# A Gram matrix from 64-column products over cyclic pairs of blocks, with one block copied by GpSimd, and an earlier load

## Chip, cores, metric

One core of a Trainium2 chip. The metric is the device time of one execution in microseconds; the kernel before takes 166.79 us in the median. Engine names in the profile lines: PE is TensorE (PEld its weight loads), ACT is ScalarE, DVE is VectorE, POOL is GpSimd, SP is SyncE. Lines such as L616 are lines of the kernel that the trace belongs to, so the same piece of code has different numbers in different kernels.

## The reference, cut to what matters

```python
# attention stand-in: a causal convolution of 7 taps over the sequence, one filter per group of 24 features
y   = conv(x, softmax(weight))                    # x: 8 batches x 4224 tokens x 192 features
# token mixer without a nonlinearity between tokens
wq, wk = y @ w_q, y @ w_k                         # 192 -> 64
W_tok  = einsum('bsd,btd->bst', wq, wk) / 8
out    = relu(W_tok @ y) @ w_out
```

Since nothing nonlinear stands between the tokens, `W_tok @ y` is `wq @ (w_k^T (y^T y)) / 8`. So the kernel needs, per batch, the Gram matrix `y^T y` (192 x 192, symmetric), its product M with w_k, the projection q of y, then `relu(q M) @ w_out`. All matmuls are in bf16.

## The kernel before

The kernel is one straight-line program. A batch has 4224 tokens; two halves of 18 chunks of 128 rows, 122 of them new. Per batch TensorE does: Y, the convolution with a banded matrix (16 matmuls of 432 columns); G, the Gram matrix, 18 chunks; Q, the projection in small tiles, from a DVE transpose of y; M; Z, `relu` input (12 matmuls of 512 columns); O, the output product. ACT and DVE move every result out of PSUM, the memory that the matmuls write into; I call such a move an eviction.

A Gram chunk, both halves in one go. Features are laid out so that three matmuls with 192, 192 and 128 columns give all blocks that are needed:

```python
    def job_g(b, c):
        def pe(e, bk):
            y = Y[:, b % 2, c, :]
            ...
            e.matmul(PS[:, 7, 0:192], y[:, 0:128], y[:, 0:192], start=c == 0, **fl)
            e.matmul(PS[:, 7, 192:384], y[:, 256:384], y[:, 192:384], start=False, **fl)
            return e.matmul(PS[:, 7, 384:512], y[:, 128:256], y[:, 128:256], start=False, **fl)
```

The last chunk of a batch has invalid rows. They are zeroed by a multiplication with a mask, on ACT or DVE (job YC):

```python
        y = Y[32:64, b % 2, NCK - 1, :]
        ... evacs=[(lambda bk: [(y, y)], ("YC", b), 140, "keep")],
```

The order of instructions on every engine is fixed when the program is built, by a list scheduler in the kernel that keeps a clock of its own. I call that the plan. It has a cost per element for ACT and DVE, and per job on TensorE:

```python
            self.pe_us = sum(max(n, 110) / 2400 + 0.0025 for n in cols)      # TensorE time of a job
    COST = {"act": (0.833e-3, 0.05, 0.16), "dve": (1.04e-3, 0.065, 0.15)}    # per element, gap, latency
            eng = min(COST, key=lambda e_: begin[e_] + n * COST[e_][0] + COST[e_][2])
```

These figures are the constants of the plan. For the evictions the trace of the kernel before agrees: from 432 to 864 columns ACT goes from 526 to 891 ns and DVE from 608 to 1052, that is 0.84 and 1.03 ns per element. The floor of 110 columns it does not show (29 ns from start to start at 64 columns, see below).

The kernel gives each engine its own list and makes it wait for the others by semaphores. The loads of x are issued by GpSimd, each batch in two halves (half loads); those for batches 2 to 7 are at the end of its list, in a ring of 6 batches.

## Time and profile before

| | before |
|---|---|
| median of runs | 166.79 us |
| span of the profiled run | 163.9 us |
| last matmul starts at | 156.5 us |
| 18 Gram chunks of a batch | 18 x 221 ns |
| TensorE idle gaps of 0.3 us or more from 30 to 120 us | 2, 0.85 us together |

The last row is worked out from the trace: start of the next matmul less start of this one, less what this one's columns take back to back. For that I take columns/2.4 + 2.5 ns, which fits the median distances of starts in this trace: 29 ns for 64 columns, 56 for 128, 83 for 192, 163 for 384, 216 for 512. I use it because the recorded matmuls overlap (those of 192 columns are 246 ns long), so that the busy time of PE hides short stops.

The head of the page and the granted clock (TensorE's clock in tenths of full speed, 9 for 90% or more, in 40 slices of the span), of the kernel before:

```profile
span 163.9 us, 4794 instructions
PE 150.9 (92%) x2017; PEld 111.6 (68%) x2017; DVE 122.0 (74%) x241; ACT 129.2 (79%) x235; POOL 51.5 (31%) x86
PEclk9999999999999999999999999999999999999995
```

Groups of TensorE instructions by shape, of the kernel before (line, engine, operation, tiles, shape, count, busy us and mean ns of one, idle before):

```profile
L619 PE MATMUL ps<-y 128*128 128x192 bf16 x144 | 33.8, 246 | 0.3 <-DVE y L884 0.3
L620 PE MATMUL ps<-y 128*128 128x192 bf16 x144 | 33.7, 246 | 0.0
L621 PE MATMUL ps<-y 128*128 128x128 bf16 x144 | 31.5, 219 | 0.0
```

The mean of 246 ns is the recorded length of one matmul. I don't take it for the cost: the next one starts after 83 ns (median), so I go by the distance of starts. The timeline of the kernel before (start us, length us, instruction) has 64-column matmuls, each with its own 128x128 weights, in the product with w_k:

```profile
40.47 0.19 PE L653 MATMUL ps<-gs,wk 128*128 128x64 bf16 x1
40.50 0.19 PE L654 MATMUL ps<-gs,wk 128*128 128x64 bf16 x1
40.53 0.19 PE L655 MATMUL ps<-gs,wk 128*128 128x64 bf16 x1
```

They start 29 ns apart (0.03 in the rounded lines). Busy times by stretch, of the kernel before: length, then busy us of each engine with its number of instructions, granted clock, share of DMA, GB/s.

```profile
25.00:40.00 15.00, 14.46 (x210) 9.84 (x203) 11.23 (x19) 12.79 (x24) 14.05 (x21) 1.00 1.51 214
40.00:60.00 20.00, 19.73 (x259) 14.15 (x259) 16.96 (x31) 18.12 (x33) 15.66 (x23) 1.00 1.41 252
80.00:100.00 20.00, 20.00 (x305) 14.78 (x304) 17.17 (x31) 17.25 (x33) 0.00 (x0) 1.00 1.30 288
```

TensorE is the fullest engine in all three, and GpSimd has nothing left to do after 62 us. The one wait of TensorE for data that is over a microsecond, from the waits view of the kernel before (total us, times, longest):

```profile
PE ps L526 <- DMA xw<-in_x_dram: 1.3, 1, 1.3
```

### The profile page before, as it was taken

How to read it: one execution, taken by the hardware profiler on the slowest of the kernel's cores; microseconds unless marked ns; L12 is line 12 of the kernel's file. 1: busy time of each engine (PE TensorE's matmuls, PEld its weight loads, DVE VectorE, ACT ScalarE, POOL GpSimd, SP SyncE). 2: the span in 40 equal slices, each digit the busy share in tenths (PEclk: the TensorE clock that was granted, in tenths of full speed). 3: DMA queues.
4: the chain of work that ended last, by engine and by line, in shares of the span. 5: the costliest groups of instructions: out<-in, count | busy, mean ns of one | idle time of the engine just before them, and what ended most of it. 6: DMA issues, size and time to landing. Idle time of an engine off the chain costs nothing.

```text
span 163.9 us, 4794 instructions
## 1 busy us (share of the span) xinstructions
PE 150.9 (92%) x2017; PEld 111.6 (68%) x2017; DVE 122.0 (74%) x241; ACT 129.2 (79%) x235; POOL 51.5 (31%) x86
## 2 busy tenths in 40 slices
PE   6899769999999999999999999999999999999920
PEld 5798637575776777777777777677777777867610
DVE  6657846696878898978796989887877987487500
ACT  4544568798999788879997988889996988799940
POOL 7984899989999541000000000000000000000000
PEclk9999999999999999999999999999999999999995
DMA  3999999999999999999999999999993473678996
GB/s 44 186 179 199 145 117 183 193 187 289 214 264 233 332 209 312 341 255 246 278 338 268 272 238 333 289 291 201 363 343 120 177 273 130 219 304 328 356 386 214
DMA packets 47894, 40.37 MB, mean 246 GB/s; under 512 B 37761, under 2 KB 39937, under 8 KB 47873
## 3 DMA queue, kind: packets, MB, share of 16 engines
q0 software_dynamic: 36544, 13.65, 70.3%
q1 hardware_dynamic: 11328, 26.42, 44.4%
q8 instruction: 16, 0.26, 0.6%
q14 instruction: 6, 0.04, 0.1%
HBM read 27.74 MB, written 25.95 MB: 328 GB/s over the span
## 4 chain that ended last, share of the span: by engine, by line
PE 73%; ACT 8%; POOL 7%; DMA 5%; issue 2%; DVE 1%; ACTq 0%; POOLq 0%
PE ps L526 12%; PE ps L733 12%; PE ps L690 11%; PE ps L735 11%; PE ps L591 8%; PE ps L619 7%; PE ps L620 6%; POOL xw L262 5%; DMA xw<-in_x_dram 5%; PE ps L621 4%; ACT o_sb L884 4%; ACT zt L887 2%; ACT y L884 1%; DVE qt L884 1%; PE ps L651 0%
## 5 line engine op out<-in xcount | busy, mean ns | idle before, releaser
L884 ACT COPY o_sb<-ps 128x768 f32<-128x768 f32 (+1 forms) x59 | 45.4, 787 | 7.2 <-PE ps L735 6.5
L884 ACT CAST y<-ps 128x864 bf16<-128x864 f32 (+7 forms) x75 | 42.7, 619 | 6.0 <-PE ps L482 4.2
L888 DVE TENSOR_SCALAR zt<-ps 128x512 bf16<-128x512 f32 x59 | 40.0, 684 | 8.1 <-PE ps L690 7.4
L733 PE MATMUL ps<-wo,zt 128*128 128x192 bf16 x256 | 42.2, 247 | 0.8 <-DVE qt L884 0.5
L262 POOL DMA_DIRECT2D xw<-in_x_dram x50 | 40.2, 817 | 6.7 <-issue 4.3
L735 PE MATMUL ps<-wo,zt 128*128 128x384 bf16 x128 | 41.7, 326 | 0.0
L733 PEld LDWEIGHTS ps<-wo,zt 128*128 128x128 bf16 x256 | 26.9, 114 | 13.0 <-issue 1.6
L882 DVE STREAM_TRANSPOSE yb<-y 128x576 int32<-128x576 int32 x48 | 34.0, 750 | 0.3
L619 PE MATMUL ps<-y 128*128 128x192 bf16 x144 | 33.8, 246 | 0.3 <-DVE y L884 0.3
L620 PE MATMUL ps<-y 128*128 128x192 bf16 x144 | 33.7, 246 | 0.0
L690 PE MATMUL ps<-qt,m_sb 128*128 128x512 bf16 x96 | 33.0, 380 | 0.0
L621 PE MATMUL ps<-y 128*128 128x128 bf16 x144 | 31.5, 219 | 0.0
L526 PE MATMUL ps<-xw,band 128*128 128x432 bf16 x112 | 29.2, 347 | 2.1 <-DMA xw<-in_x_dram 1.3
L884 DVE CAST y<-ps 128x864 bf16<-128x864 f32 (+10 forms) x33 | 19.7, 628 | 7.1 <-PE ps L526 3.9
L887 ACT ACTIVATE zt<-ps 128x512 bf16<-128x512 f32 x37 | 21.6, 619 | 0.6 <-PE ps L690 0.5
L884 ACT CAST qt<-ps 128x576 bf16<-128x576 f32 (+1 forms) x21 | 11.8, 584 | 9.0 <-PE ps L591 9.0
L620 PEld LDWEIGHTS ps<-y 128*128 128x128 bf16 x144 | 14.1, 98 | 6.1
L619 PEld LDWEIGHTS ps<-y 128*128 128x128 bf16 x144 | 14.1, 98 | 5.2 <-issue 1.5
L884 DVE CAST qt<-ps 128x234 bf16<-128x234 f32 (+1 forms) x27 | 10.2, 414 | 9.6 <-PE ps L591 9.6
L591 PE MATMUL ps<-yb,wq 32*64 32x288 bf16 x768 | 15.4, 285 | 0.4 <-ACT y L884 0.4
L526 PEld LDWEIGHTS ps<-xw,band 128*128 128x128 bf16 x112 | 9.2, 97 | 7.8 <-DMA xw<-in_x_dram 1.5
L735 PEld LDWEIGHTS ps<-wo,zt 128*128 128x128 bf16 x128 | 14.5, 113 | 0.0
(79 smaller groups left out, 137.3 us busy)
## 6 DMA issues: line engine op xcount, KB each, us to landing
out_dram<-o_sb SPq DMA_DIRECT2D x31, 768.0 KB, 7.0
xw<-in_x_dram POOLq DMA_DIRECT2D x21, 384.0 KB, 22.8
xw<-in_x_dram POOLq DMA_DIRECT2D x7, 432.0 KB, 21.7
xw<-in_x_dram POOLq DMA_DIRECT2D x4, 240.0 KB, 5.4
out_dram<-o_sb SPq DMA_DIRECT2D x16, 48.0 KB, 5.8
out_dram<-o_sb SPq DMA_DIRECT2D x2, 384.0 KB, 3.6
xw<-in_x_dram POOLq DMA_DIRECT2D x8, 42.0 KB, 10.7
xw<-in_x_dram POOLq DMA_DIRECT2D x1, 336.0 KB, 7.8
```

The lines of the kernel that those rows point to most:

```text
L262: return e.dma_start(XW[lo:hi, b % NX, half, c : c + n, :], bass.AP(x_t, at, [[D, hi - lo], [CW * D, n], [1, D]]),)
L526: last = e.matmul(PS[:, k + j, 0 : 48 * n], BAND[:, h, :], rhs, start=True, stop=True)
L591: last = e.matmul(PS[64 * h : 64 * h + 64, bk + i, 0:288], WQ[r, j, :], rhs, start=j == 0, stop=j == 5, skip_group_check=True)
L619: e.matmul(PS[:, 7, 0:192], y[:, 0:128], y[:, 0:192], start=c == 0, **fl)
L620: e.matmul(PS[:, 7, 192:384], y[:, 256:384], y[:, 192:384], start=False, **fl)
L621: return e.matmul(PS[:, 7, 384:512], y[:, 128:256], y[:, 128:256], start=False, **fl)
L690: return e.matmul(PS[:, bk, :], m[:, parts[k] : parts[k] + 128], q, start=True, stop=True)
L733: e.matmul(o[:, 192 * h : 192 * h + 192], z[:, h, cols], WO1[:, :], start=h == 0, stop=False, **kw)
L735: last = e.matmul(o[:, 0:384], z[:, 2, cols], WO2[:, :], start=False, stop=True, **kw)
L882: return e.transpose(o, i)
L884: return e.copy(o, i) if eng == "act" else e.tensor_copy(o, i)
L888: return e.tensor_scalar(o, i, 0.0, None, op0=ALU.max)
```

## The change

The intent: use the symmetry. With three blocks A, B, C of 64 features, the weights AB, BC and CA, each with its first block as the 64 moving columns, give the six blocks that are needed. Six matmuls of 64 columns replace three of 192, 192 and 128: 384 columns instead of 512. The kernel reads each pair's weights as one run of 128 columns, so for CA it puts a copy of A behind C. That copy (job D, 64 of 192 features) is made by DVE for batches 0 and 1 and by GpSimd afterwards. The mask moves to GpSimd too from batch 2 on. Loads are issued from within the list: three batches up front, then half a batch in front of each copy. The second half load of batch 1 moves ahead of the casts of w_k and w_out.

The core of the diff:

```diff
-    NX = 6
+    NX = 5
+    AHEAD = 3
-    Y = sbuf("y", [128, 2, NCK, 2 * D], BF16)
+    Y = sbuf("y", [128, 2, NCK, 2, YW], BF16)          # YW = 256: 192 features and the copy of 64
     load(1, 0)
+    load(1, 1)
     ...
-            self.pe_us = sum(max(n, 110) / 2400 + 0.0025 for n in cols)
+            self.pe_us = sum(n / 2400 + 0.0025 for n in cols)
     ...                                                 # evictions of y: one piece instead of three
+    def job_dup(b, g):
+        def make(bk):
+            o, i = (Y[:, b % 2, c0:c1, hs, d0 : d0 + 64].rearrange("p c h d -> p h c d")
+                    for d0 in (D, 0))
+            return [(o, i)]
+        return Job(
+            ("D", b, g), ykey(b, c1), 0, None, [],
+            reads=[("Y", b, g, k) for k, q in enumerate(heads) if q[0] < 3]
+            + [("YC", b)] * (c1 == NCK),
+            evacs=[(make, ("D", b, g), 64 * n * len(halves), "dup")],
+        )
     ...
-            e.matmul(PS[:, 7, 0:192], y[:, 0:128], y[:, 0:192], start=c == 0, **fl)
-            e.matmul(PS[:, 7, 192:384], y[:, 256:384], y[:, 192:384], start=False, **fl)
-            return e.matmul(PS[:, 7, 384:512], y[:, 128:256], y[:, 128:256], start=False, **fl)
+            for h in range(2):
+                y = Y[:, b % 2, c, h, :]
+                for k in range(3):
+                    last = e.matmul(
+                        PS[:, 7, 64 * k : 64 * k + 64], y[:, 64 * k : 64 * k + 128],
+                        y[:, 64 * k : 64 * k + 64], ...
     ...                                                 # product with w_k: six matmuls of 64 columns
+    EASY = {"act": 1.0, "dve": 0.3, "pool": 2.0}        # planned cost of copy and mask, relative
     def place(job, t):
+        if kind == "D" and job.name[1] > 1:
+            prefetch(job.name[1] + AHEAD, job.name[2])
+            if what in ("dup", "keep"):
+                if key[1] > 1:
+                    eng = "pool"
```

## The prediction

> What bounds it now. From about 30 to 153 us TensorE is the limit. The busy table by windows gives PE 20.0 of 20 us from 60 to 140 us, ACT 16-18, DVE 16-17.5. Busy PE is no proof, so I read start-to-start times in the timeline: matmuls follow each other at columns/2.4 + 2.5 ns (192 columns 83 ns, 128 56 ns, 512 216 ns), and no gap over 0.45 us is left there. A batch costs 17.5 us (projection bursts of L591 at 70.0, 88.0, 105.1, 122.9 us). Before 30 us the input DMA limits: PE waits 1.3 us for xw at 21.0 us (waits view). After 156.5 us only stores remain, 7 us.
>
> Removed on PE. A Gram chunk is 192+192+128 columns: 83+83+56 = 221 ns. Then it is six 64-column matmuls with a weight load each. The trace has such pairs: L653, L654, L655 and L693 start 29 ns apart with 128x128 weights. So 6 x 29 = 175 ns, 46 less, x18 = 0.83 us per batch. The product with w_k falls from 281 to about 175 ns; the transpose stays. Together 0.93 us per batch. [...]
>
> Removed elsewhere, per batch: the split evictions of one head pair (432+144+288 elements, 0.53+0.29+0.43 us on ACT) become one of 0.89, twice: 0.7 us. The Gram eviction shrinks from 512 to 192 columns: 0.60 to 0.33. The masking of y (0.61 on ACT) goes to GpSimd. About 1.6 us off ACT+DVE (about 30 per batch): they keep pace with the faster PE.
>
> Added. A copy of 1152 elements per half batch: on GpSimd about 1.2 us (estimate from its casts, 288 ns for 128 and 347 for 192 columns)[...]. GpSimd issues loads at 0.5-1.0 us each until 62 us, then idles. The copies wait in its queue behind at most one half load (2.5-3 us), while a batch's Gram starts several us after its y: mostly hidden. [...]
>
> Moved. The second half load of batch 1 is issued at 19.4 us, after the casts; the DMA queue nearly runs dry at 20-22 us. Now it is issued at about 13.7 us, and the casts end about when they did. It should land some 2 us earlier, but PE does not wait for it now, and the wait at 21.0 us is for the first half, which stays. So the Gram saving of batch 0 is lost in that wait, and the move is worth 0 to 1 us. A ring of 5 instead of 6 is still far ahead of need.
>
> Critical path: 7 batches x 0.93 = 6.5 us plus 0.1. Result 160.3 us, 8 in 10 between 158.5 and 162.5. Faster by over 2%: 0.93; within 2%: 0.06; slower: 0.01.
>
> Right if: 64-column Gram matmuls start 29 ns apart; projection bursts of one kind come 16.5-16.7 us apart; PE has no large gaps from 30 us on; GpSimd copies take 1-1.5 us; the wait at 21 us remains, longer.
>
> Wrong if: six weight loads in a row cost more than 29 ns each (37 ns wipes out the gain); PE waits for GpSimd copies around 45-60 us, when loads still fill that queue; DVE becomes slower beside GpSimd; or the earlier load shortens the start by over 1 us.

7 x 0.93 and 0.1 are 6.6 us, which from 166.8 leave 160.2 (put down as 160.3). The distances of starts that the sum rests on are those of the trace of the kernel before, 83, 56 and 29 ns in the median. The queue that nearly runs dry is in its windows view: a DMA share of 0.28 from 20.0 to 20.5 us and 0.03 from 20.5 to 21.0.

## The result, and the profile after

The changed kernel takes 167.74 us in the median (167.47 to 167.91), before 166.79. The ratio is 1.0067, with a 95% interval from 1.0044 to 1.0089: within 2% of before, and a little slower. (Ratios in this text are the mean time of one kernel's fast runs over that of the other's fast runs in the same rounds, so not quite the ratio of the medians quoted.) I had predicted 160.3 us.

The head of the page of the changed kernel:

```profile
span 165.7 us, 5636 instructions
PE 144.4 (87%) x2453; PEld 105.5 (64%) x2453; DVE 120.4 (73%) x231; ACT 124.5 (75%) x212; POOL 74.3 (45%) x104
PEclk9999659999999999999999999999999999999998
```

PE has less to do, and ACT and DVE too, as predicted; the span is longer all the same. So time was lost in waiting. Two groups of the page are new, and one in the groups by shape, of the changed kernel:

```profile
L616 PE MATMUL ps<-y 128*128 128x64 bf16 x864 | 36.7, 195 | 5.3 <-POOL y L890 2.6 <-DVE y L890 2.5
L890 POOL COPY y<-y 128x1152 bf16<-128x1152 bf16 x12 | 13.8, 1153 | 3.8 <-ACT y L890 1.7 <-DVE y L890 1.6
L896 POOL TENSOR_SCALAR y<-y,keep 32x384 bf16<-32x384 bf16 x6 | 7.4, 1240 | 59.1 <-DVE y L890 46.4 <-ACT y L890 12.7
```

The 64-column Gram matmuls start 29 ns apart (median of 801 pairs), so a chunk costs 175 ns as predicted. The copies take 1.15 us each, near the estimate of 1.2. But the Gram matmuls now stand idle for 5.3 us, 5.1 of it behind copies (2.6 on GpSimd, 2.5 on DVE), and the mask takes 1.24 us on GpSimd. Busy times by stretch, of the changed kernel:

```profile
25.00:40.00 15.00, 12.10 (x205) 7.11 (x182) 12.45 (x23) 11.86 (x19) 14.18 (x22) 1.00 1.53 181
40.00:60.00 20.00, 18.31 (x387) 13.60 (x383) 15.81 (x30) 15.27 (x24) 13.77 (x16) 1.00 1.40 258
80.00:100.00 20.00, 17.47 (x307) 12.91 (x307) 14.52 (x27) 15.41 (x26) 6.02 (x6) 1.00 1.35 271
```

In each of these stretches PE is below the value of before. TensorE gaps of 0.3 us or more from 30 to 120 us are now nine, 8.3 us together, where there were two and 0.85 us. I found three kinds.

**The start.** All engines in the timeline of the changed kernel, lines that matter:

```profile
16.11 0.34 PE L616 MATMUL ps<-y 128*128 128x64 bf16 x6
...
17.23 1.44 DVE L888 STREAM_TRANSPOSE yb<-y 128x576 int32<-128x576 int32 x2 [0.53 <-ACT y L890]
17.28 0.61 ACT L896 ACTIVATE y<-y,keep 32x384 bf16<-32x384 bf16 x1
...
18.59 0.45 DVE L890 COPY y<-y 128x448 bf16<-128x448 bf16 x2
...
19.10 0.82 PE L616 MATMUL ps<-y 128*128 128x64 bf16 x12 [2.49 <-DVE y L890]
```

The last two copies of batch 0 wait for the mask (17.28) and stand behind two transposes in DVE's list. The Gram stops for 2.5 us. The record of the granted clock goes to half at 17.42 us and back at 24.25. In the kernel before it stayed full until 160.4 us. The first matmul of Z, which needs the whole Gram matrix of batch 0, starts at 29.05 us instead of 25.06.

**The queue of GpSimd.** The timeline of the changed kernel around 88 us:

```profile
85.90 1.24 POOL L896 TENSOR_SCALAR y<-y,keep 32x384 bf16<-32x384 bf16 x1 [10.99 <-DVE y L890]
...
87.20 1.82 POOL L263 DMA_DIRECT2D xw<-in_x_dram  x2
...
89.01 0.68 POOL L279 DMA_DIRECT2D xw<-in_x_dram  x1
...
89.73 2.42 POOL L890 COPY y<-y 128x1152 bf16<-128x1152 bf16 x2
...
90.93 0.70 PE L616 MATMUL ps<-y 128*128 128x64 bf16 x18 [1.73 <-POOL y L890]
```

y was there at 85.9 us. The copy that the Gram needs was done at 90.9: mask, half a load, copy, one after the other. The same happens at 43.7 us for the first copy on GpSimd, behind the loads of batches 2 to 4 and the first half load of batch 5. Plan and trace disagree there by 11 us: the plan has this copy at 32.7 us, because it counts no time for issuing loads. It starts at 43.58.

**The order of evictions.** Three more stops of about 1 us have no copy in them. The timeline of the changed kernel at 79.5 us:

```profile
79.49 0.25 PE L696 MATMUL ps<-qt,m_sb 128*128 128x64 bf16 x3
79.65 0.80 ACT L890 COPY o_sb<-ps 128x768 f32<-128x768 f32 x1
...
80.51 0.39 PE L693 MATMUL ps<-qt,m_sb 128*128 128x512 bf16 x1 [0.77 <-ACT o_sb L890]
```

The next Z matmul is to go into a PSUM bank that ACT only now empties. It happens at 47.9, 79.5 and 99.4 us (at 99.4 us the profile names an eviction on DVE, `zr`, instead), each time behind the three small matmuls of the last 64 rows (L696).

Theories, as I held them before the experiments: A, the copies and the waits for them ate the gain. B, the new order of work, and evictions in it, leave TensorE idle, copies or not. C, the small matmuls are slow when they go on for long.

### The profile page after: what moved, and what is told of

Its sections match the earlier page's. It is cut to its first block, busy times and chain, and to the rows that moved or that the text cites. A ratio compares the mean times of both kernels' runs of the same rounds, so it can differ in the third digit from the quotient of the medians.

```text
span 165.7 us, 5636 instructions
## 1 busy us (share of the span) xinstructions
PE 144.4 (87%) x2453; PEld 105.5 (64%) x2453; DVE 120.4 (73%) x231; ACT 124.5 (75%) x212; POOL 74.3 (45%) x104
## 3 DMA queue, kind: packets, MB, share of 16 engines
q1 hardware_dynamic: 11472, 26.45, 43.8%
## 4 chain that ended last, share of the span: by engine, by line
PE 55%; POOL 28%; ACT 8%; issue 4%; DVE 2%; ACTq 0%; POOLq 0%
POOL xw L263 18%; PE ps L616 12%; PE ps L693 9%; PE ps L736 9%; PE ps L738 9%; PE ps L517 9%; PE ps L587 6%; ACT o_sb L890 6%; POOL xw L279 2%; POOL y L890 1%; ACT zt L893 1%; POOL wk L790 1%; POOL xw L444 1%; POOL y L896 1%; ACT zr L893 1%
## 5 line engine op out<-in xcount | busy, mean ns | idle before, releaser
L890 ACT COPY o_sb<-ps 128x768 f32<-128x768 f32 (+1 forms) x63 | 47.3, 779 | 4.4 <-PE ps L738 3.5
L890 ACT CAST y<-ps 128x864 bf16<-128x864 f32 (+4 forms) x50 | 39.7, 811 | 10.7 <-PE ps L517 6.6
L894 DVE TENSOR_SCALAR zt<-ps 128x512 bf16<-128x512 f32 x56 | 37.6, 683 | 9.1 <-PE ps L693 9.0
L616 PEld LDWEIGHTS ps<-y 128*128 128x128 bf16 x864 | 33.5, 100 | 14.6 <-POOL y L890 3.2
L616 PE MATMUL ps<-y 128*128 128x64 bf16 x864 | 36.7, 195 | 5.3 <-POOL y L890 2.6
L896 POOL TENSOR_SCALAR y<-y,keep 32x384 bf16<-32x384 bf16 x6 | 7.4, 1240 | 59.1 <-DVE y L890 46.4
L890 DVE CAST y<-ps 128x864 bf16<-128x864 f32 (+3 forms) x22 | 20.5, 933 | 8.2 <-PE ps L517 5.7
L890 DVE CAST qt<-ps 128x234 bf16<-128x234 f32 (+1 forms) x31 | 11.9, 423 | 15.8 <-PE ps L587 15.8
L890 POOL COPY y<-y 128x1152 bf16<-128x1152 bf16 x12 | 13.8, 1153 | 3.8 <-ACT y L890 1.7
L693 PEld LDWEIGHTS ps<-qt,m_sb 128*128 128x128 bf16 x96 | 8.9, 97 | 8.1 <-ACT o_sb L890 1.8
## 6 DMA issues: line engine op xcount, KB each, us to landing
xw<-in_x_dram POOLq DMA_DIRECT2D x21, 384.0 KB, 19.8
```

What stands on the lines that cost most here:

```text
L616: last = e.matmul(PS[:, 7, 64 * k : 64 * k + 64], y[:, 64 * k : 64 * k + 128], y[:, 64 * k : 64 * k + 64], start=c + h + k == 0, stop=c == ...
L693: return e.matmul(PS[:, bk, :], m[:, parts[k] : parts[k] + 128], q, start=True, stop=True)
L890: return e.copy(o, i) if eng == "act" else e.tensor_copy(o, i)
L894: return e.tensor_scalar(o, i, 0.0, None, op0=ALU.max)
L896: return e.mul(o, i, s) if eng == "act" else e.tensor_scalar(o, i, s, None, op0=ALU.mult)
```

## Experiments

Medians and ratios of fast runs. One run of e_late (166.92 us) and one of e_costs_ahead2 (165.56 us) were slow and are left out; with them the medians are 166.24 and 162.13 us. "Before" ran in the same rounds (about 166.1 to 166.4 us in the median in these). I compare the ratios.

| run | median us | ratio to before (95%) |
|---|---|---|
| e_nodup (wrong result) | 161.91 | 0.9752 (0.9698 to 0.9806) |
| e_tiles | 188.56 | 1.1379 (1.1321 to 1.1438) |
| e_dfirst | 165.80 | 0.9998 (0.9941 to 1.0055) |
| e_before_early | 165.74 | 1.0009 (0.9953 to 1.0064) |
| e_start0 | 170.28 | 1.0234 (1.0168 to 1.0300) |
| e_plan | 167.25 | 1.0055 (1.0011 to 1.0100) |
| e_start_dfirst | 163.25 | 0.9809 (0.9752 to 0.9867) |
| e_best2 | 163.76 | 0.9863 (0.9810 to 0.9916) |
| e_late | 165.69 | 0.9951 (0.9855 to 1.0047) |
| e_start | 164.13 | 0.9864 (0.9794 to 0.9934) |
| e_costs_np | 162.08 | 0.9748 (0.9684 to 0.9812) |
| e_late_ahead2 | 165.14 | 0.9920 (0.9842 to 0.9998) |
| e_unmask1 | 170.36 | 1.0236 (1.0182 to 1.0290) |
| e_yc_act | 171.43 | 1.0320 (1.0275 to 1.0366) |
| after_again | 167.75 | 1.0089 (1.0051 to 1.0128) |
| e_costs_ahead2 | 161.83 | 0.9730 (0.9681 to 0.9779) |
| e_costs_d2 | 163.35 | 0.9807 (0.9770 to 0.9845) |
| e_before_costs | 171.10 | 1.0271 (1.0232 to 1.0309) |

A caution for all of them: most edits change what the scheduler sees, and then the order on every engine changes too, and with it which evictions ACT does and which DVE. Only some pairs have the same order on PE, ACT and DVE, so that one thing alone differs: the changed kernel and e_dfirst; e_start and e_start_dfirst; e_start_dfirst and e_late; e_late and e_late_ahead2; e_costs_np and e_costs_ahead2; the kernel before and e_before_early.

### No copies: e_nodup and e_tiles

e_nodup:

```diff
-            evacs=[(make, ("D", b, g), 64 * n * len(halves), "dup")],
+            evacs=[],
-            + [("D", b, g) for g, q in enumerate(GROUPS[b]) if q[1] <= c < q[2]]
-                        PS[:, 7, 64 * k : 64 * k + 64], y[:, 64 * k : 64 * k + 128],
+                        PS[:, 7, 64 * k : 64 * k + 64], y[:, 64 * min(k, 1) : 64 * min(k, 1) + 128],
```

> Wrong result on purpose: the changed kernel without the copies; the third block pair takes columns that are already there as its weights, so TensorE does the same number and shapes of matmuls and nothing waits for a copy. Theory A (the copies and the waits for them ate the gain: the 2.5 us wait at 16.5-19 us, and the waits for GpSimd at 43.7 and 88.9 us): about 160.5 us. Rival B (the new order of work and the evictions, not the copies, leave TensorE idle: the gaps after the small matmuls at 48, 80 and 100 us): 165 to 167 us, with those gaps still there. Rival C (sustained 64-column matmuls are slow): still 167-168 us.

161.91 us. So C falls: the same matmuls are as fast here. The timeline of e_nodup has six of them in 0.34 us at 29.02 us, as long as six take in the changed kernel at 16.11 us. The distance to the changed kernel is 0.9752 against 1.0067, about 5 us of the 7.4 that the prediction missed. It is A together with whatever the other order is worth: none of the stops after the small matmuls is left in this order. The head of the page of e_nodup, and the largest stop that is left in its timeline:

```profile
span 160.7 us, 5636 instructions
PE 144.2 (90%) x2458; PEld 103.8 (65%) x2458; DVE 113.1 (70%) x218; ACT 128.2 (80%) x216; POOL 60.3 (38%) x92
32.38 0.54 PE L517 MATMUL ps<-xw,band 128*128 128x432 bf16 x2 [2.14 <-issue]
```

The profile puts this stop, 2.3 us at 30.0 us by my measure, down to nothing ("issue"); it comes back below. One more of 1.4 us, at 122.8 us, stands behind transposes on DVE.

e_tiles gets the right result without a copy, from two matmuls with 64-column weights:

```diff
+            for h, k, p, q, w in (
+                (0, 0, 0, 128, 0), (0, 1, 0, 128, 64), (1, 0, 0, 128, 0), (1, 1, 0, 128, 64),
+                (0, 2, 0, 64, 128), (0, 2, 64, 128, 0), (1, 2, 0, 64, 128), (1, 2, 64, 128, 0),
+            ):
+                y = Y[:, b % 2, c, h, :]
+                last = e.matmul(PS[p:q, 7, 64 * k : 64 * k + 64], y[:, w : w + q - p],
+                                y[:, 64 * k : 64 * k + 64], ...)
```

> Right result without any copy: the third pair is made by two matmuls with 64-column weights that land in the two halves of the partitions. If two such matmuls run side by side as the projection's small ones do (starts a few ns apart) and changing between full and half-width weights costs nothing, as e_nodup: about 160.5 us under theory A. [...] a chunk costs 0.2 us more, that is 3.6 us per batch: 185 us or more.

The trace of the kernel before shows: the first matmul of a projection burst (64-column weights) starts 149 ns or more after a 128-column Gram matmul, where another full-width one starts after 56, and the first after a burst starts 210 to 212 ns after the last of 288 columns, for which columns/2.4 + 2.5 gives 122. So about 0.1 us for each change of width.

188.56 us. The two half-width matmuls do run side by side (starts 4 ns apart), but the change of width costs: starts in one chunk are 29, 29, 29, 123, 4, 49, 3 and 129 ns apart, 395 ns in all (the median of 85 chunks is 404), where the six of the change take 175. So a change between 128- and 64-column weights costs about 95 to 100 ns each way here (123 and 129 less 29), as at the projection bursts.

### The queue: e_dfirst and e_plan

In e_dfirst the half load is issued after the copy instead of before it:

```diff
-        if kind == "D" and job.name[1] > 1:                 # at the top of place()
-            prefetch(job.name[1] + AHEAD, job.name[2])
+        if kind == "D" and job.name[1] > 1:                 # at its end
+            prefetch(job.name[1] + AHEAD, job.name[2])
```

> The changed kernel, but each GpSimd copy is put ahead of the next half load in GpSimd's queue. Theory A: the copies start 2.5-3 us earlier, the GpSimd waits of TensorE (1.05 us at 43.7, 1.9 us at 88.9) vanish: 164.5 to 166 us, the start unchanged. Rival B: 167-168 us, gaps move elsewhere.

165.80 us, and TensorE no longer waits for GpSimd. PE, ACT and DVE have the same order as in the changed kernel, so this is the queue alone: 1.0067 (or 1.0089 in the repeat) to 0.9998, 0.7 to 0.9%, about 1.2 to 1.5 us. By the intervals in the table the difference is uncertain by about 0.6 to 0.7% either way, so it is only just clear of noise. The first copy on GpSimd starts at 41.5 instead of 43.6 us. The stops at the start and after the small matmuls are all still there.

e_plan corrects the plan instead: it counts the loads and the measured durations on GpSimd.

```diff
+    free["pool"] = 40.6                                    # when the early loads have been issued
+            free["pool"] += (3.05, 2.55)[part]             # per half load
+                n *= (1.15 if what == "dup" else 3.7) if eng == "pool" else EASY[eng]
```

> The changed kernel with its own planning clock corrected for GpSimd: it counts the issue of loads (about 2.5 and 3 us per half) and the measured 1.15 us per copy and 1.24 us per mask; instructions are the same, only the order differs. If TensorE's idle times from 30 to 110 us come from a plan that takes GpSimd to be free when it is issuing loads (planned start of the first GpSimd copy 32.7 us, measured 43.6): gaps behind GpSimd vanish and the time is about 165.5 us. If the real wait for the copies is the limit whatever the order: 167 us or more.

167.25 us. The waits for GpSimd vanish here too, and others take their place: 0.87 us at 46.9, 0.68 at 49.4, 1.15 at 97.6, 1.11 at 115.8 us. A plan that knows of the late copy puts off the Gram, but does not make the copy earlier.

### The start: e_start0, e_start, e_start_dfirst, e_unmask1

e_start0, batch 0 only: copies don't wait for the mask. The mask comes afterwards and covers the copied columns as well, and transposes queue behind the copies.

```diff
-            + [("YC", b)] * (c1 == NCK),
+            + [("YC", b)] * (c1 == NCK and b > 0),
-        y = Y[32:64, b % 2, NCK - 1, :, 0:D]
+        wide = YW if b == 0 else D
+        y = Y[32:64, b % 2, NCK - 1, :, 0:wide]            # and the mask of batch 0 reads its copies
+            + [("D", 0, g) for g, q in enumerate(GROUPS[0]) if b == 0 and k > 2 ...]   # transposes
```

> The changed kernel with the start of batch 0 alone mended: its copies no longer wait for the mask (the mask covers the copied columns afterwards instead), and its transposes queue behind the copies on DVE. If the start is a large part of the loss (TensorE idle 2.65 us at 16.4 us, then at half clock until about 24 us, first use of the product with w_k at 29.05 us against 25.06 before): the half clock after 20 us is gone, the first matmul of L693 comes at about 25 us and the time falls by 2 to 3 us against the changed kernel, to about 165 us. If the start is caught up later anyway: 167 us or more.

170.28 us: slower than the change. The wait for the copies at the start is mended: the first Z comes at 25.08 us, and there is no half clock at 17 us. The half clock is not gone, as I had expected, though: the record shows it from 23.16 to 26.57 us, after a stop of 2.5 us at 21.0 us that the changed kernel does not have (see below). And TensorE then reaches the Gram of batches 2 to 5 earlier, and GpSimd does not have the copies earlier (43.8, 53.9, 58.0 us). From the waits of e_start0, where the changed kernel has 2.6 us:

```profile
PE ps L620 <- POOL y L894: 6.1, 4, 2.2
```

The time that was won at the start is handed to the next wait, and a stop of 2.3 us at 71 us is followed by half clock once more (3.4 us from 74.4).

e_start does in all batches what e_start0 does in batch 0 (mask after copy; the edit of the transposes stays one of batch 0); e_start_dfirst adds the order of e_dfirst:

```diff
-            reads=[("Y", b, g, k) for k, q in enumerate(heads) if q[0] < 3]
-            + [("YC", b)] * (c1 == NCK),
+            reads=[("Y", b, g, k) for k, q in enumerate(heads) if q[0] < 3],
-            reads=["keep"] + yreads(b, [NCK - 1]),
-            evacs=[(lambda bk: [(y, y)], ("YC", b), 384, "keep")],
+            reads=["keep"] + yreads(b, [NCK - 1])
+            + [("D", b, g) for g, q in enumerate(GROUPS[b]) if q[2] == NCK],
+            evacs=[(lambda bk: [(y, y)], ("YC", b), 512, "keep")],
```

> e_start_dfirst without the last of its edits: the half load stands ahead of the GpSimd copy again; copies still don't wait for the mask. If the queue position is what makes TensorE wait for GpSimd (6.1 us in e_start0, none in e_start_dfirst): waits of 3 us or more, 166 to 168 us. If leaving out the wait for the mask was what helped: 163 to 164 us.

> No copy waits for its mask in any batch (the mask follows the copies and covers them), transposes of batch 0 behind its copies, and each GpSimd copy ahead of the next half load. If start and GpSimd queue add up: about 163 to 164 us. If they overlap: 165 us or more.

164.13 and 163.25 us, neither with a wait for GpSimd. I had expected e_start to need the better queue position as well: a miss. Once the copy leaves the mask behind it, half a load in front of it does little harm (0.5% between the two, of the size of the intervals). Between e_start0 and e_start lie 6 us and the 6.1 us of waits for GpSimd; the orders differ, so that the two numbers agree is no proof.

e_unmask1 is the complement of e_start0, mask after copy from batch 1 on and the start untouched:

```diff
-            + [("YC", b)] * (c1 == NCK),
+            + [("YC", b)] * (c1 == NCK and b == 0),           # and the wide mask for b > 0
```

> The changed kernel with one edit, from batch 1 on only: the second copy of a batch no longer waits for the mask (the mask follows and covers the copied columns). Batch 0 and its start as in the change. If the chain mask, half load, copy on GpSimd is what TensorE waits for: no wait for GpSimd from 50 us on, about 165 to 166 us. If the start alone decides: 167.5 us or more.

170.36 us, a miss again. Its order puts the Gram of batch 2 early, and TensorE stands 5.3 us at 39.3 us in front of the first copy on GpSimd, which starts at 43.6 us behind the early loads. After that no wait for GpSimd follows. From its waits:

```profile
PE ps L618 <- POOL y L892: 5.2, 1, 5.2
```

So each half of the repair alone made the kernel slower by some 1.5%, and both together (e_start) made it 2.0 to 2.2% faster than the change; with the copy ahead of the half load as well (e_start_dfirst) it is 2.6 to 2.8%.

### One part undone: e_yc_act and e_before_early

e_yc_act puts the mask back on ACT or DVE:

```diff
-                if key[1] > 1:
+                if key[1] > 1 and what == "dup":
```

> The changed kernel with one part undone: the mask is again done by ACT or DVE, as before, instead of GpSimd (1.24 us there, 0.61 on ACT). If the mask on GpSimd is what delays the second copies: the waits for GpSimd of 1.9 us at 89 us go, about 166 us. If ACT's time is dearer than that: 168 us or more.

171.43 us, a miss. The long waits for GpSimd go down to 0.9 us in total, but the order is another, with stops of 0.8 to 1.0 us at ACT's evictions in every batch from the sixth on (100.4, 107.9, 118.8, 126.4, 137.3 us). Since the order differs, this run does not show what the place of the mask costs by itself. e_start leaves the mask on GpSimd and has no wait for GpSimd, which points to what has to wait for the mask.

e_before_early is the kernel before with the early load alone:

```diff
     load(1, 0)
+    load(1, 1)
     warm(20, [])
```

> The kernel before, with only the second half load of batch 1 moved ahead of the weight casts. If the early load is harmless or worth little (prediction): 166 to 167 us, second half landing 2 us earlier. If it is part of the loss (it delays the casts and with them the product with w_k): 168 us or more.

1.0009: nothing, as predicted, in a kernel that does not wait for this load.

### Is the early load worth anything? e_late, e_late_ahead2 and a stop that the profile puts down to nothing

In e_start_dfirst TensorE stops at 21 us. The timeline of its matmuls, and then of its weight loads:

```profile
20.90 0.35 PE L517 MATMUL ps<-xw,band 128*128 128x432 bf16 x1
23.55 0.71 PE L517 MATMUL ps<-xw,band 128*128 128x432 bf16 x3 [2.30 <-issue]
```

```profile
20.88 0.12 PEld L517 LDWEIGHTS ps<-xw,band 128*128 128x128 bf16 x2
```

Two matmuls belong to one job here, with no semaphore between them. The weights of the second were loaded at once, its matmul came 2.65 us later. The granted clock stayed full through this stop (PEclk is 9 in every slice of the page but the last), where in e_start0 stops of 2.5 and 2.3 us were followed by half clock, so these runs give no threshold. In this gap a transfer of the instruction queue starts, at 21.2 us. The early load keeps the 16 DMA engines full until 24 us. (The changed kernel issues the same load early: its DMA share in the windows view is 1.6 from 18 to 24 us, and 1.03 from 24 to 25.) The same pattern, a stop labelled "issue" with a transfer of instructions beginning at it, stands in e_nodup (30.0), e_start, e_start0 and e_best2 (21.0). e_late issues the load after the casts, as before, and e_late_ahead2 also loads two batches ahead instead of three:

```diff
     load(1, 0)
-    load(1, 1)
     warm(20, [])
     ...
     cast("wo", WO2S[:, :], WST[:, 3, :], [wl[2]])
+    load(1, 1)
-    AHEAD = 3
+    AHEAD = 2                                              # e_late_ahead2 only
```

> e_start_dfirst with one part of the change undone: the second half load of batch 1 is issued after the weight casts again. In e_start_dfirst TensorE stops for 2.47 us at 20.9 us between two matmuls of one job, with nothing to wait for by the profile, and a transfer of instructions starts at 21.2 us, about 2 us later than in the kernel before. If the early load fills the DMA engines and holds up that transfer: it starts near 19.5 us again, the 2.4 us gap is gone or moved, and the time is about 161 to 162 us. If the gap has another cause: it stays, 163 us or more.

> e_late with two batches loaded ahead instead of three: GpSimd reaches the first copy about 6 us earlier. If any wait for the first copies is left in e_late: faster by up to 1 us. If not: the same as e_late within 0.5 us.

165.69 and 165.14 us, worse than 163.25. The transfer of instructions does start earlier (19.6 and 20.1 us) and the stop shrinks from 2.47 to 0.74 and 1.04 us, so that part of the theory held. But the load itself is now late. The waits of e_late_ahead2 (its profile is of a fast run, that of e_late of a slow one, with the same wait of 2.5 us):

```profile
PE ps L516 <- DMA xw<-in_x_dram: 2.7, 2, 2.6
```

So, by this reading, the early load costs about 1.5 us by holding up instructions (2.47 against 0.74 and 1.04) and saves about 2.6, and only in a kernel that is fast enough to need it. In ratios it is 0.9809 against 0.9951, with intervals that overlap a little; the fast runs of e_late alone lie between 164.34 and 166.79 us. So a net gain is likely and not clear of noise.

That the late instructions are the cause of the stop is inferred; the profile does not name it. But counting supports it well. In the six traces with this stop at 21 us (the two of e_late among them) exactly 705 recorded instructions of TensorE, weight loads and waits counted, come before it. In e_nodup 961 come before the stop at 30.0 us, and the shorter stops labelled "issue" near 15 us, in eight traces, all come after 449. These counts are 256 apart, and there is about one transfer of 16 KiB for every 256 of TensorE's instructions (16 transfers for 4094 recorded ones in the kernel before, 19 for 4951 in the changed one). Each of these stops ends 1.2 to 1.6 us after such a transfer has ended. The kernel before and e_before_early, which have the same order, show the early load's part: the transfer starts at 19.4 us in the one and at 21.3 in the other. There it costs nothing, as TensorE gets to its 705th instruction only at 28.5 us (counted in the trace of the kernel before).

### A better plan: e_best2, e_costs_np, e_costs_ahead2, e_costs_d2, e_before_costs

e_best2 is e_start_dfirst with the corrected GpSimd times in the plan and two batches ahead (the two edits shown above, with 34.0 us instead of 40.6):

> As e_start_dfirst, with the corrected planning clock and with two batches loaded ahead instead of three, so that GpSimd has issued its early loads by about 34 us instead of 40.6. If the queue before the first copy and the plan are what is left: 161.5 to 163 us, ahead of both kernels. If the loads of batch 4 then come late: a DMA wait before its first matmuls and 164 us or more.

163.76 us, nothing gained over e_start_dfirst. e_costs_np leaves GpSimd's plan alone and puts measured times for the evictions in pieces and for the DVE copies into it:

```diff
-                  ("M", b, 0), 192, "scale"),
+                  ("M", b, 0), 310, "scale"),
-                  ("M", b, 1), 250, "scale"),
+                  ("M", b, 1), 390, "scale"),
-                  ("Z", b, i, 0), 370, "relu"),
+                  ("Z", b, i, 0), 640, "relu"),
-    EASY = {"act": 1.0, "dve": 0.3, "pool": 2.0}
+    EASY = {"act": 1.3, "dve": 0.62, "pool": 2.0}
```

> e_start_dfirst with measured costs in its planning clock for the evictions in several pieces (relu of the last 64 rows 0.65 us instead of 0.36, product with w_k 0.75 instead of 0.47) and for copies on DVE; the same instructions in another order. If the stalls of up to 1.3 us that follow those evictions come from a plan that takes them to be short: they vanish, 161.5 to 162.5 us. If not: within 0.5 us of e_start_dfirst.

162.08 us, as expected, and the stops after the small matmuls are gone. The head of its page:

```profile
span 160.0 us, 5646 instructions
PE 141.9 (89%) x2436; PEld 107.2 (67%) x2465; DVE 117.9 (74%) x232; ACT 124.8 (78%) x211; POOL 75.7 (47%) x104
PEclk9999999999999999999999999999999999999995
```

One wait of 2.17 us for the first copy on GpSimd is left, at 39.2 us. Two runs were to take it away:

> e_costs_np with two batches loaded ahead instead of three, so that GpSimd reaches its first copy about 4 us earlier. In e_costs_np TensorE waits 2.17 us at 39.2 us for that copy, which starts at 40.3 us after the loads. If that wait is what is left: gone, 160 to 161 us, as predicted for the change. If the time is set elsewhere: 162 us.

161.83 us: the wait is gone and nothing is gained. (That it is gone is read from a profile of a slow run, so I draw no more from it.) In e_costs_d2 the first copy of batch 2 is made by DVE:

```diff
-                if key[1] > 1:
+                if key[1] > 1 and key[1:] != (2, 0):
```

> e_costs_np with one copy more on DVE, the first of batch 2, which on GpSimd starts only at 40.3 us behind the early loads and makes TensorE wait 2.17 us. If that wait is real time lost: gone, 160 to 161 us. If the time is set elsewhere (e_costs_ahead2 took the wait away and gained nothing): 162 us.

163.35 us: the wait is gone, and in the order that results the stops after the small matmuls are back (0.55, 1.01, 1.18, 1.18 us). Where the last 2 us to the predicted time go is left open. The pace is nearly the predicted one: from 45 to 129 us the projection bursts of one kind come 16.7 to 17.1 us apart in e_costs_np; I had predicted 16.5 to 16.7, and in the kernel before they are 17.1 to 17.9 from 53 us on.

Would the plan have helped the kernel before? e_before_costs makes the same three edits there (310, 390, 640):

> The kernel before with the same corrected planning costs as e_costs_np, so that its gain is not mistaken for one of the change. If the better plan needs the lighter TensorE work to pay: 166 to 167 us. If the plan alone is worth as much in the kernel before: 164 us or less.

171.10 us: 2.7% slower, with a kernel whose matmuls, copies and loads are those of before. Its waits:

```profile
PE ps L690 <- ACT o_sb L884: 3.3, 4, 0.8
```

These are four stops of 0.98 us by my measure from start to start (the waits view counts 0.8 of each as idle), each behind the small matmuls of the last 64 rows, of the same kind as in the changed kernel. So B is shown to be possible: an order alone, with the division of the evictions between ACT and DVE that comes with it, can cost 4.5 us, about what the change gained without its copies (e_nodup), and no copy is needed for it.

### The change once more

> The changed kernel once more, on the same chip and in the same rounds as the others of this call, as the measure for single edits: 167 to 168 us, ratio 1.00 to 1.01 to the kernel before.

167.75 us, 1.0089. The profile has the same stops at 16.5, 44.1, 47.8, 79.4, 88.8 and 99.4 us.

## Why the prediction was wrong

- **Cost of the matmuls: right.** 29 ns per 64-column matmul with its weights, 175 ns per chunk. The fit to the kernel before, columns/2.4 + 2.5 ns, gives 29.2 for 64 columns, and the changed kernel has 29 from one to the next (median of 801 pairs). Once the stops end, the pace shows it as well: after the last one, at 100.7 us, the changed kernel's projection bursts of one kind come 16.1 to 17.0 us apart, before that 15.9 to 19.8 (from 50 us on).
- **Relief of ACT and DVE: right.** Summed over the instructions, evictions of y fell by 6.1 us, those of the Gram matrix by 2.2 and the mask by 3.7 (it stays on ACT for two batches): 1.5 us per batch, where I had 1.6. DVE's copies took 2.9 us of it back. Busy time, in which overlaps count once, fell less: by 4.7 us on ACT and 1.6 on DVE over the span (129.2 to 124.5, 122.0 to 120.4).
- **"Critical path: 7 batches x 0.93": this step failed.** I took TensorE's saved time as saved time, because TensorE was full. It did do less (PE's busy time fell by 6.5 us, from 150.9 to 144.4), but its gaps of 0.3 us and more from 30 to 120 us grew from 0.85 to 8.3 us. A full engine only hands its savings on if everything that it waits for comes earlier as well.
- **"The copies wait behind at most one half load ... mostly hidden": failed.** I costed the copy (1.2 us; 1.15 measured, about 1.0 ns per element) but not what stands before it. The first one stood behind the loads of batches 2 to 4 and half of batch 5 until 43.6 us, and the second of each batch behind the mask, 1.24 us on GpSimd, and in batches 2 to 4 also behind half a load. I had booked the mask as relief for ACT (0.61 us) and had not costed it on GpSimd at all (those 1.24 us are for 384 elements; the 512 of e_start take 1.56). My list of what could go wrong did name waits for copies at 45 to 60 us; I gave it too little weight. e_dfirst puts the queue position alone at 1.2 to 1.5 us.
- **"The wait at 21 us remains ... the Gram saving of batch 0 is lost in that wait": failed.** It assumed that the start could not get worse. It did: copies on DVE behind the mask and two transposes stopped TensorE for 2.5 us, and the clock went to half for 6.8 us. The first Z came 4 us late. But mending it alone (e_start0) made the kernel slower, so these 4 us can't be booked as a loss that adds to the others.
- **"The move is worth 0 to 1 us": right for a kernel that does not need it** (e_before_early, 1.0009), and probably too low for one that does: about 1.4% in e_start_dfirst against e_late, not clear of noise.
- **"DVE becomes slower beside GpSimd": some copies do, and it is small.** The copy of 1152 elements takes DVE between 0.42 and 0.89 us. In all 13 cases over 0.55 us in these traces it ends 0.27 to 0.31 us after the instruction that GpSimd was at (the issue of a load, once a memset) has ended. In the changed kernel the copy at 26.28 us takes 0.83 us and ends 0.28 us after such an issue; that at 38.14 us takes 0.42, with an issue under way all the time. The loss is at most 0.5 us per copy, and DVE makes such copies for batch 1 alone in most of the kernels.
- **Not in the prediction at all: the order.** The change alters the planned times, and with them the order of every engine's list. Orders with the same work spread over several per cent: e_before_costs lies 2.7% above before, which is clear; e_costs_np lies 0.6% below e_start_dfirst, which is within the intervals. About 3 us of the gaps in the changed kernel (47.9, 79.5, 99.4 us) are of this kind. I had read the diff's change from `max(n, 110)` to `n` as bookkeeping; no run undoes it alone, so how much of the new order comes from it and how much from the new jobs is open. The ring of 5 and the loads within the list were not undone alone either, but TensorE waits for no load after 20.6 us in the trace of the changed kernel.

A split of the 7.4 us into start, queue and order can't be given: the parts are not additive (e_start0, e_unmask1). What is shown is that without copies the gain of the matmuls appears (e_nodup, 2.5% below before), that with copies most of it appears once they neither wait for the mask nor stand behind transposes (e_start and e_start_dfirst, 1.4 and 1.9% below before), that it is 2.5% with the plan's eviction costs put right as well (e_costs_np), and that the queue position alone is worth under 1%.

e_costs_np beats both kernels: 162.08 us, 0.9748 of the kernel before with an interval from 0.9684 to 0.9812, with the right result.

## What to carry to other kernels

When work is taken off a full engine and small new work is put on an idle one, cost the queue of the idle engine and not only the new instruction: what stands before it, and what each thing there has to wait for. In a kernel whose order is fixed by a planner, treat each change of a cost as a new order, compare only pairs with the same order for causes, and expect swings as large as the gain. A repair that makes the kernel slower may still be half of the right one, if the time it frees runs into the next wait.
